# Attention then mixture of experts on one core: exponentials written in the order in which they are read, router lists with row and token apart

## The chip, the core and the metric

One core of a Trainium2 chip runs the whole program as one launch. The metric is the time of one execution in microseconds (us), as the device measures it. The engines are named as in the profile: PE (TensorE, matmuls), PEld (TensorE's weight loads), DVE (VectorE), ACT (ScalarE), POOL (GpSimd) and SP (SyncE, which here only issues DMAs). "Clock" is the granted clock of TensorE as a share of its upper level.

## The reference

Two parts, one behind the other. Attention: q and k are normalised by row (RMS with gains), then softmax(q k^T / 8) v for 8 batches of 12 heads, 448 positions, 64 numbers a head. Its output is laid out as 3584 tokens of 768 numbers. Then a mixture of 8 experts, of which each token goes to one:

```python
q_n, k_n = (rmsnorm(q, g_q), rmsnorm(k, g_k))
scores = scale * np.matmul(q_n, k_n.transpose(0, 1, 3, 2))
attn = np.exp(scores - np.max(scores, axis=-1, keepdims=True))
attn = attn / (np.sum(attn, axis=-1, keepdims=True) + 1e-09)
x = np.matmul(attn, v)   # 8, 12, 448, 64 -> 3584 tokens x 768
logits = x @ w_gate      # 8 experts, 448 tokens each, best logit first
for e in range(8):
    out[mask_e] = np.maximum(x[mask_e] @ w1[e], 0) @ w2[e]
```

## The kernel before

Attention works in 24 groups g of four heads (three groups make a batch of 12 heads). All its work is cut into tasks, and a task has one engine. `Plan.run` issues the tasks in the order of a long table of digits, `ORDER`; two tasks of one engine therefore run in the order of the table, whatever is ready first. A planner with task durations (`US`, in which an exponential has 0.917) made the table outside the program. Each task waits for its inputs by semaphores.

For a group, in order: SP loads q, k and v (`load_qk`, `load_v`); ACT squares (`square`, line 301) and DVE sums (307); ACT and POOL make the reciprocal roots (313 to 321); POOL normalises (342) and multiplies by the gains (371); ACT writes the upper halves of the numbers as f16 (376) and POOL the rest (379); SP issues two DMA transposes (389, upper halves into kqh, lower into kql). Then PE makes scores with the upper halves for the row maxima (`max_score`, 504; DVE reduces them, 514), small transposes of the maxima (444) go back as a row through a DMA (456), and PE makes the exact scores, transposed, keys on partitions (`scores`, 535 and 537; 542 and 544 for the first groups).

One unit d is a seventh of a group: 16 matmuls into the PSUM tile psc (128 x 896), then one exponential on ACT (`exp`, 553) from psc into the SBUF tile e (128 x 896 f32). There are 168 units. `av` (572) then uses 64-column pieces of e as weights and v as the moving operand; a call is one window w of seven, 8 matmuls in the program and 16 in the profile, since those in f32 show twice. There are 336 such windows. DVE and ACT normalise the result po (585 to 605) into xa, and once per batch SP stores xa to the DRAM scratch xd (`x_store`) and transposes it for the gate (612); gate matmuls (668 to 676) make the logits.

Groups 0 to 2 are loaded so that a partition holds three neighbouring tokens of a head, and groups from 3 on (`seven(g)`) so that a partition holds seven. A column 64 j + i of psc then is token 7 i + j. For these 147 units `exp` writes e through a view that puts column 64 j + i at place 7 i + j, so that neighbouring elements are written 28 bytes apart and e stands in token order. For the first 21 units input and output are both dense.

psc has two buffers, e has 15, kqh 4, kql 3. All exponentials run on ACT, beside squares, upper halves, part of v's copies and one of the steps on po.

`Router` places tokens. Its constants are made during attention on POOL and DVE (`later`); `tok` holds the token of each partition and column in two parts, number / 64 and the rest, since bf16 holds no more. Phase k fills the expert that is full at that point: `at`, `columns` and `rows` make one-hot operands, `lists` multiplies them on PE (28 matmuls of 8 columns) and two DVE instructions put the parts together to `idx`. `Experts.gather` reads rows of xd by idx (an indirect DMA on POOL), and `result` scatters its rows to the output by the same idx. Phase 0 stands between attention and the first expert; the others run beside the experts before.

Of the kernel before, what the change touches and what calls it, by code (L numbers as in the profile page):

```python
# [89 lines left out]
class Attention:  # L90
# [792 lines left out]
    def plan_first(self, plan, g, a):  # L883
# [51 lines left out]
        "Bw2bL-LyBxRBBy3fGu2F3M2dM22G2e2H2f3O3Q2g2IRCM4BzB+M6GvB-M5GxRD3g3hC0RERFC1M3M8M7C23N3P3i3j3k4M3R4NGw3+Gy3-C3Gz"
        "C4H140G+C5C6G-353637C7C8413l38H0H23m0A0B3n3o4243M9MBMFC9CAH5H3CBH4H6RGRHCCRIRJ4O4QMAMEMCCDCEMDRKH7H8CFCGH9HA3p"
        "44464548473Z3q3rMGCHMKMHMMML4RCICJ4P4SCKRLRMHB4THDHCHE3S3TMJCLHFMI4U49RNROCMCNHGRPRQCOHHHJCPRRCQRSMNMPMRCRCS4A"
        "4V4B3V4W4X3WHIHK4mRTRU583UHNHL3X4o4YHMCTCUMTMUMXCV4nCW5AHO4a4p4q3Y4rMQMaMOMW594CCXCYMSHP3sRVRW3t3uRXMYCZCaMVHR"
        "CbCcMZ3z5CRYHQHSHTCdRZRaRbCe5BHVHUHWMbMgCfCgRcHX4c4b3v4Z4D4dHZHYChCiMhMcMfCj5DCkHbRdHaHcReRhRjHdHe5E5FClCmMeMd"
        "Mi4E4F4G0C4s0DRtHfCnCoRuMoMjMmCpRvCq4u4t4w4v4x3x5Y4y4zHhHgHlCrCsHiRw3yRxMlMnMkRyCtCuHjHkHm3wMpMvCvMtMuMs5ZRzCw"  # L940
        "Cx5G5H5I5JR+CyHnHpR-5aHoS04e4f5bMrMqRl4+CzS1C+Hq5c5dHrHsRi5w5K5y5M4LRgRk5x4H4I5eHt4JHuC-D0S2MwMxMyD1D20rS3S4Mz"
        "M-N0D3D4HvHwS55L5NHxD5D6M+S65z4gRm4h5fHyHzH+D7D8S7S8H-RnRoRpD9DA4jI04KS9SAI1I2I35ODBDCRqN1N250514-Rf4k5iI5DDRr"
        "RsDEN3N8NDDF5g5hI45k5j0E5l4iDGI6NBN5NEDJDKI7I9DH5+5-6KI8IA606M61DIN4N6N7SBNA0FSCDLDMSDIBICSE526i5mIDDNDON9SFIF"
        "4lDPDQNCSG6L0G626465630H0I0J535654IEIGNFNHNI5QSH5RSISJIHIIDRDSSKNJIJ5P666768IKDTDU6N6ONGNKNLSZDVNMNQNRNO5n6j5S"
        "DWDXDYILINSaSbDZDa6P6k556mIMScSdIONSNPNN0K0L6Q6R69575T6S6TDbDc6nIPIR5WIQ6UIS5o5p6l6oNTNUNZSPSS6ADdITIU76DeSeSf"
        "SgShIV6p6WIW6XDfDgSiNYNXNWNVDhSjDiSkIXSRSQSTSVSUDjSlDkIZIYSmIbSnDlDmSWIa78SX77SYNaNgNcDnDoIdNb5V5UNhDp79Dq5qSL"
        "IcIe6YIfIhIg7AIiDrNeDs6B5X6q6V6s6r6tNfNkNd6CSo6DSpSq7B6u6wSr5r6xSO5vIj7U7V7W5tIk5uDtDuSsNlNnIlDxDyNoNjNpDvDwNm"
        "NiNqStDzInImIoIpD+SuSvSwD-E0SxNtNsIrE1Nr7XE25sNvNuSy6y7YIqNyNzN-6a6ESMSN6ZIt6v0M7C7D0N0O7E7u7G6J8G6z7F0P0Q7H6F"
        "SzS+S-Is6b6cT0T4T5T87I7KT6T7E3E46G0R6IN+NwNxO0O3TF7ZTGE5Iv6HIuIwTH7a7b7wTIE67vO4IxE7E8IzO5O2O1IyI+7x7yEBECI-J3"
        "E9J0TJEAO6J17J8H7LT2EDEETK7c0S7d7e8I7f6d6eJ2O7ODO8OAJ4EFJ56f7gJ68JTLTMTNO9J7EG6+6-T370J9EH7zJ8JA7i7k7j7h7+80TO"  # L950
        "EIOCOBTPTQTRTSJBEJEKJDT9TBTAELTTEMJCJEJFJHEPEQJGJI6gOETCOKOJENEO8KTDTEJLJJERESJKJM7-82818485OGOHOIOFETOLONOP6h"
        "718LEU8M8N8O0T0U72EVEWTUTVJN8gJOJPJQ7M7N9275T1937l7OTWOMEXEYTXTYOQJRJSEZOOOREaOSEbTZEcTaTb8i7374OTOUOYEdEeTcTd"
        "JTJV838P8Q8687Ef8ROVOWOX7PJU7SJW7ROZOfOeEgTe8hTfTgEhJZEiObOa7m7n7oJX8S8TTh8U8VJYJa94Ti7TTnTpTk8WEjEkOcOgOiOd8j"
        "TxTyElEmTzJbJcJdJeEnEoT+T-OhOjOkOlOmEpEq95U0JfJgJhErEsU1U27Q7p7s8k96Ji8l8m8oOnOoOqOrEtEuJjJkJlJmEvOpEwJp8889U3"
        "U4JnEx97EyOtOuOsOxOvO+U5EzU6U7E+Jo8nJq8p8q8sU89S8tU9JrJtJsJuE-F07tTqOzOyOw8BUAUBToTlTrTsTtUCF1F2JxUD98997r8EJv"
        "Jw9UUEF3Tu7q8rO-P0P3P4TvJyF49TTwF5P1F6P6P7F7F89q8XTj8A8uJzJ+8DJ-K0F99V9WFAP5PCP9P2FBFCUFUGK1K38F8v9r9A9B9C9E9D"
        "9GK2K48Y8Z8a9IPAUHFFFGK5K7FDUI9XUJFE9H8C9Y9a9FP8PBPDUKULUM9sK6K8PFFHFIUNUOUTUWUUKBK9KAKCFJFKPEPJPKFLFMKDKEKFFN"
        "FOPQKHKGKI9u8w8x8yTm8fUSKJKK9Z8b9c8d9b8e9eFPPGPOPPFQFRFS9tPHPMPIFVFWUdUeKLUfKNKMKOUgPNFTFUUhKRKPKQFXPL9d8c8z9f"
        "90KS8+9v9w9xFYPRPWPUPTFZUiUjFaKTKUUkUl8-KVKW9gFbFcAEUmPXPSPVUn9K9LUoKXFdKZ91UVUXUZUYUpFeFfUqUrUaUbPYPZPeFgKYUc"
        "FhFiAF9y9+9-9z0V0WAc9JA0A2Ad9hKaAGAeA19MA49RPfPjPiFjFkAHAIAJPdPbPcPa0X9NA3AKAM9OFlFmUsUtKbA5KdFnPgPlPkPhFoUu9i"  # L960
        "9jUR9kKcKeUvKfKgKhKiFpUxUyUwFqUzU+PmPsPrPnFrFsKjKlFtU-AfFuPoPpPqV0V1V2AgAhKk9P9QPtPwPuPyFvFwKnPxPz0YALANAOAQV3"
        "V40Z0a9lAiAjKmKo9n9m0bAPAk0c0d0eAlARAmAnFxFyKpKqB0KrKsFzF+UPUQPvVJP+Q1F-G0VKKtKvAS9pG1G2AoAp9oKuKwVLVMQ2Q0Q3A6"
        "A7B1VNKzKxG3G4V7V8V9VBVAQ4P-A9ABKyAqA8K+Q5Q7Q6QBVOVPVQG5G6K-L1VRACVSG9GAB2B3Q8QAQ9VTG7G8L0L2B4B5QCQFQEQDGBVUVV"
        "GCL3L5GDGEQGQIQHVWVXL4L6VCATAsGFVYVZGGL7L9L8LAAUAVVaVDVEVFGHGIVbVcLBLDGJVGB6B7ArB8AAB9ADAXAYAZLCAaBABCBDBBVHAW"
# [11 lines left out]
class Router:  # L976
# [23 lines left out]
    def __init__(self, ctx, tc, logits):  # L1000
# [61 lines left out]
        tok = c.tile([128, NT], I32, name="tok")  # L1062
        for b, n in ((0, 1), (1, 5), (6, 1), (7, 1)):
            i, m = self.column(b)
            later("P", 0.13, G.iota, tok[:, i:i + 3 * n].rearrange("p (b j) -> p b j", j=3),
                  pattern=[[448, n], [128 if b else 1, 3]], base=448 * b, channel_multiplier=1 if b else 3)
            if b in (0, 6):
                n = 1 if b else 3
                for h in range(2):
                    later("P", 0.13, G.iota, tok[64 * h:64 * h + 64, m:m + n], pattern=[[896, n]],  # L1070
                          base=448 * (b + h) + 384, channel_multiplier=1)
        part = c.tile([128, 2, NT], I32, name="tokp")
        later("D", 0.1, V.tensor_scalar, part[:, 0], tok, 6, None, op0=OP.logical_shift_right)
        later("D", 0.1, V.tensor_scalar, part[:, 1], tok, 63, None, op0=OP.bitwise_and)
        self.tok = c.tile([128, 2, NT], BF, name="tokb")
# [912 lines left out]
```

## Time and profile before

| | us |
|---|---|
| median of 3 runs (969.11 to 973.3) | 970.84 |
| the profiled execution | 970.76 |
| its span, first to last instruction | 968.7 |
| first exponential starts | 32.57 |
| last `av` matmuls start | 463.83 |
| first gather of rows starts | 493.56 |

Attention fills about the first 464 us, phase 0 of the router with little matmul work follows, and from 500 us on PE is busy nearly without a break with the experts. A row with a count ("x4") groups instructions of one kind that stand together. Matmuls are pipelined: the distance between two starts tells what PE needs for the work between them, and the duration of a row contains a tail in which the next one already runs.

### The profile page before, as it was taken

The numbers are of one execution on the slowest core, as the hardware profiler recorded it, in microseconds if no ns is written. First come the engines' busy times: TensorE is split into PE (matmuls) and PEld (weight loads), VectorE is DVE, ScalarE is ACT, GpSimd is POOL, SyncE is SP. The second block draws the span as 40 slices with busy tenths as digits, with TensorE's granted clock in tenths as the row PEclk, the third lists the DMA queues.
The fourth block names the chain that finished last, engine by engine and source line by source line (L and its number), as shares of the span: only waits on it lengthen the run. The fifth ranks groups of instructions, "written<-read, shape, count | busy, mean of one in ns | idle before, by whom it ended". The sixth has DMA issues, their size and how long they took to land.

```text
span 968.7 us, 30160 instructions
## 1 busy us (share of the span) xinstructions
PE 876.6 (90%) x13219; PEld 584.3 (60%) x13220; DVE 658.9 (68%) x1457; ACT 583.9 (60%) x670; POOL 342.8 (35%) x421
## 2 busy tenths in 40 slices
PE   2799889898998898888679999999999999999996
PEld 1466656675765676667555655556555565555783
DVE  6988777776776676653679677777775858338640
ACT  4889999999998999887224342434242414333421
POOL 6778656775745576510010202111101111020101
PEclk9999999999999999999679999999999999999999
DMA  6586869798896687391163756968684929660501
GB/s 190 151 169 151 178 132 214 174 222 166 180 197 146 116 204 153 58 223 26 60 219 100 234 174 196 236 193 224 197 212 149 268 81 293 222 139 8 181 17 41
DMA packets 224951, 157.30 MB, mean 162 GB/s; under 512 B 162100, under 2 KB 211508, under 8 KB 224820
## 3 DMA queue, kind: packets, MB, share of 16 engines
q1 hardware_dynamic: 219378, 132.90, 57.3%
q0 software_dynamic: 4608, 22.02, 6.6%
q8 instruction: 103, 1.69, 0.7%
q10 hardware_dynamic: 834, 0.46, 0.2%
q14 instruction: 28, 0.23, 0.1%
HBM read 94.40 MB, written 22.02 MB: 120 GB/s over the span
## 4 chain that ended last, share of the span: by engine, by line
issue 33%; PE 10%; POOL 5%; DVE 2%; DMA 0%; ACT 0%; POOLq 0%; DVEq 0%
PE ph L1765 6%; PE py L1782 3%; POOL out_dram L1798 3%; POOL rows L1702 3%; DMA rows<-xd,idx 0%; PE rp L1238 0%; POOL spacer L1797 0%; PE rp L1466 0%; PE rp L1309 0%; DVE or L1213 0%; DVE or L1459 0%; DVE cmp L1223 0%; PE py L1791 0%; PE py L1717 0%; ACT xt L1721 0%
## 5 line engine op out<-in xcount | busy, mean ns | idle before, releaser
L553 ACT ACTIVATE e<-psc 128x896 f32<-128x896 f32 x168 | 275.8, 1715 | 19.8 <-PE psc L537 15.7
L514 DVE TENSOR_REDUCE mx<-pm 128x2 f32<-128x896 f32 x162 | 176.6, 1090 | 69.4 <-PE pm L504 66.8
L572 PEld LDWEIGHTS po<-v,e 128*64 128x64 f32 x5376 | 168.5, 138 | 39.5 <-issue 33.1
L572 PE MATMUL po<-v,e 128*64 128x65 f32 x5376 | 185.9, 224 | 7.1 <-ACT e L553 2.6
L1765 PE MATMUL ph<-xt,w1h 128*128 128x448 f16 (+2 forms) x708 | 183.5, 343 | 0.4 <-DVE xt L1723 0.3
L1798 POOL DMA_INDIRECT out_dram<-y,idx x32 | 34.2, 1070 | 307.3 <-ACT y L1784 238.0
L1782 PE MATMUL py<-w2h,hh 128*128 128x384 f16 x384 | 125.0, 326 | 0.0
L1782 PE MATMUL py<-w2h,hl 128*128 128x384 f16 x384 | 125.0, 326 | 0.0
L1782 PE MATMUL py<-w2l,hh 128*128 128x384 f16 x384 | 125.0, 325 | 0.0
L1765 PE MATMUL ph<-xt,w1l 128*128 128x448 f16 (+2 forms) x354 | 119.9, 343 | 0.0
L1754 ACT ACTIVATE hh<-ph 128x448 f16<-128x448 f32 x56 | 30.5, 544 | 121.9 <-PE ph L1765 107.5
L1782 PEld LDWEIGHTS <-hh 128*128 128x128 f16 x768 | 73.6, 97 | 45.6
L1765 PEld LDWEIGHTS <-w1h 128*128 128x128 f16 x708 | 64.8, 97 | 52.7 <-issue 1.5
L1784 ACT ACTIVATE y<-py 128x384 f32<-128x384 f32 x48 | 23.5, 490 | 116.0 <-PE py L1782 92.5
L535 PE MATMUL psc<-kqh 64*64 64x448 f16 x588 | 56.2, 362 | 36.2 <-ACT e L553 33.1
L535 PEld LDWEIGHTS <-kqh 64*64 64x64 f16 x1176 | 44.1, 107 | 62.7 <-issue 49.0
L1702 POOL DMA_INDIRECT rows<-xd,idx x32 | 31.5, 986 | 115.4 <-DVE idx L1472 46.8
L1569 DVE SCALAR_TENSOR_TENSOR w2l<-stage,w2h 128x768 f16<-128x768 f32 x64 | 60.3, 952 | 10.7 <-ACT w2h L1565 10.6
L379 POOL TENSOR_TENSOR s<-qn,s 128x896 f16<-128x896 f32 (+2 forms) x25 | 44.6, 1786 | 47.5 <-ACT s L376 23.2
L504 PE MATMUL pm<-kqh 64*64 64x448 f16 x588 | 56.7, 364 | 2.5 <-DVE mx L514 2.1
L379 POOL TENSOR_TENSOR s<-kn,s 128x896 f16<-128x896 f32 (+2 forms) x25 | 44.7, 1787 | 34.2 <-ACT s L376 32.4
L307 DVE TENSOR_REDUCE st<-sq 128x14 f32<-128x910 f32 (+2 forms) x52 | 52.6, 1018 | 5.5 <-ACT sq L301 5.4
(301 smaller groups left out, 1640.2 us busy)
## 6 DMA issues: line engine op xcount, KB each, us to landing
stage<-in_moe_w_dram SPq DMA_DIRECT2D x64, 768.0 KB
vraw<-in_v_dram SPq DMA_DIRECT2D x21, 448.0 KB
xd<-xa SPq DMA_DIRECT2D x16, 576.0 KB
qkraw<-in_q_dram SPq DMA_DIRECT2D x10, 896.0 KB
qkraw<-in_k_dram SPq DMA_DIRECT2D x10, 896.0 KB
xd<-xa SPq DMA_DIRECT2D x16, 96.0 KB
vraw<-in_v_dram SPq DMA_DIRECT2D x3, 384.0 KB
qkraw<-in_q_dram SPq DMA_DIRECT2D x2, 384.0 KB
```

Of the source, the lines that this page charges most:

```text
L307: self.nc.vector.tensor_reduce(self.stat(g, 0, a)[:, i], self.view(self.T["sq", g, i], a), axis=AX.X, op=OP.add)
L379: self.tt("lo" + name, g, a)(self.half(g, 1, name, a), self.flat(self.T[name + "n", g], a), self.half(g, 0, name, a), op=OP.subtract)
L504: self.nc.tensor.matmul(o, mine, self.every(k, r, a), start=True, stop=True)
L514: self.nc.vector.tensor_reduce(m, p[r, :, :448], axis=AX.X, op=OP.max)
L535: mm(o, mine, self.every(q, r, n), start=i == 0, stop=False)
L553: self.nc.scalar.activation(e, p, AF.Exp, scale=scale)
L572: self.nc.tensor.matmul(po[o:o + 64, w], self.T["e", d][:, h, q:q + 64], self.v32[g % 2][:, h, 4 * a + d % 7 % 4], start=d == ds[0], stop= ...
L1569: self.later(0.93, lambda w=w: self.nc.vector.scalar_tensor_tensor(l[:, w], v[:, w], self.WS, h[:, w], op0=OP.mult, op1=OP.subtract), k, i)
L1702: nc.gpsimd.indirect_dma_start(out=g[:n, c, :], out_offset=None, in_=self.xd, in_offset=bass.IndirectOffsetOnAxis(ap=idx[:n, c:c + 1], axi ...
L1765: nc.tensor.matmul(p, a, b[:, o], start=st, stop=sp)
L1782: nc.tensor.matmul(p, a[:, f, s], b[:, f, o], start=st, stop=sp)
L1798: st = nc.gpsimd.indirect_dma_start(out=self.out, out_offset=bass.IndirectOffsetOnAxis(ap=self.router.idx[k][:n, c:c + 1], axis=0), in_=y[ ...
```

## The change

`exp` loses its view: all 168 exponentials read psc and write e in psc's own order. For groups from 3 on, place 64 j + i of e now holds token 7 i + j, so xa and the rows of xd stand in that order. For batch 0, `x_store` writes rows in the form of the other batches. So the row of a token in xd is no longer its number. `tok` therefore holds two lists, row and token (four parts), made by 20 iotas in place of 9; `columns` makes a one-hot and one product over all four parts in place of two products; the matmuls of `lists` have 16 columns in place of 8, and two more DVE instructions make a second list. `gather` goes by the row, `result` by the token. `ORDER` is a new table, since tasks were added.

```diff
@@ exp
-        p = p[:, :, :448]
-        if self.seven(d // 7):
-            e, p = e.rearrange("p h (i j) -> p h j i", j=7), p.rearrange("p h (j i) -> p h j i", j=7)
-        self.nc.scalar.activation(e, p, AF.Exp, scale=scale)
+        self.nc.scalar.activation(e, p[:, :, :448], AF.Exp, scale=scale)
@@ x_store
-            o = xd[:384].rearrange("(j p) (h c) -> p j h c" if b else "(p j) (h c) -> p j h c", j=3, h=2)
+            o = xd[:384].rearrange("(j p) (h c) -> p j h c", j=3, h=2)
@@ ORDER
-        "030500040708090n0v0x0w0y0o0p0602110z0-0+101213141Q151R16171S181A01191B1T1U1C1V1D1W2l1t1s1r1u1y2K1w1v1+1P1Y1X1E"
+        "050204031506160z1718191A0+1B0708000-1C1E1G1c1F1H1d1I1J1e1K1f1L091g1h1i1N1D1b1M011P1R242122252326281k1j1O1Q2x2z"
...
@@ Router.__init__
-        tok = c.tile([128, NT], I32, name="tok")
+        tok = c.tile([128, 2, NT], I32, name="tok")
...
-        later("P", 0.2, G.tensor_copy, self.tok, part)
+        later("D", 0.1, V.tensor_scalar, part[:, :, 0], tok, 6, None, op0=OP.logical_shift_right)
+        later("D", 0.1, V.tensor_scalar, part[:, :, 1], tok, 63, None, op0=OP.bitwise_and)
+        self.tok = c.tile([128, 4, NT], BF, name="tokb")
+        later("P", 0.3, G.tensor_copy, self.tok, part.rearrange("p n i t -> p (n i) t"))
@@ columns
-            V.tensor_tensor(oa[:, 0], ar[:, 0, :, None].to_broadcast([128, NT, 4]),
+            V.tensor_tensor(one, ar[:, 0, :, None].to_broadcast([128, NT, 4]),
                             self.row[:, None, 0:4].to_broadcast([128, NT, 4]), op=OP.is_equal)
-            for i in (1, 0):
-                V.tensor_tensor(oa[:, i], oa[:, 0], self.tok[:, i, :, None].to_broadcast([128, NT, 4]), op=OP.mult)
+            some = [128, 4, NT, 4]
+            V.tensor_tensor(oa, one[:, None].to_broadcast(some), self.tok[..., None].to_broadcast(some), op=OP.mult)
@@ lists
-            q = p[:, 0:8].rearrange("p (i a) -> p i a", i=2)
+            q = p[:, 0:16].rearrange("p (i a) -> p i a", i=4)
...
-            lo = self.small("idlo", [128, 4])
-            V.tensor_copy(lo, q[:, 1])
-            idx = self.idx[k] = self.w.tile([128, 4], I32, name="idx", bufs=8)
-            V.scalar_tensor_tensor(idx, q[:, 0], 64.0, lo, op0=OP.mult, op1=OP.add)
+            for n, of in enumerate((self.idx, self.out)):
+                lo = self.small("idlo", [128, 4])
+                V.tensor_copy(lo, q[:, 2 * n + 1])
+                idx = of[k] = self.w.tile([128, 4], I32, name=f"idx{n}", bufs=8)
+                V.scalar_tensor_tensor(idx, q[:, 2 * n], 64.0, lo, op0=OP.mult, op1=OP.add)
@@ result
-            out=self.out, out_offset=bass.IndirectOffsetOnAxis(ap=self.router.idx[k][:n, c:c + 1], axis=0),
+            out=self.out, out_offset=bass.IndirectOffsetOnAxis(ap=self.router.out[k][:n, c:c + 1], axis=0),
```

ACT in the middle of attention, around the third batch's gate (lsc is its part on ACT, s1 the f16 halves, st the roots, sq the squares), before:

```order
L553 ACTIVATE e_4527<-psc_4443 128x2x7x64
L553 ACTIVATE e_4529<-psc_4466 128x2x7x64
L553 ACTIVATE e_4571<-psc_4531 128x2x7x64
L553 ACTIVATE e_4573<-psc_4548 128x2x7x64
L467 ACTIVATE v32_1_139<-vraw_1_135 64x2x3x64
L301 ACTIVATE sq_1_137<-qkraw_3986 128x14x64
L707 ACTIVATE lsc_4620<-po_4483 128x24
L708 ACTIVATE lsc_4620<-po_4483 64x8
L553 ACTIVATE e_4665<-psc_4642 128x2x7x64
L553 ACTIVATE e_4667<-psc_4625 128x2x7x64
L376 ACTIVATE s1_4671<-kn_4669 128x896
L376 ACTIVATE s1_4671<-qn_4418 128x896
```

The same place now:

```order
L596 ACTIVATE xa_4120<-po_4220 128x7x64
L550 ACTIVATE e_4550<-psc_4516 128x896
L301 ACTIVATE sq_0_136<-qkraw_4403 128x14x64
L550 ACTIVATE e_4604<-psc_4533 128x896
L704 ACTIVATE lsc_4606<-po_4471 128x24
L705 ACTIVATE lsc_4606<-po_4471 64x8
L301 ACTIVATE sq_1_137<-qkraw_4403 128x14x64
L301 ACTIVATE sq_0_136<-qkraw_4403 128x14x64
L550 ACTIVATE e_4658<-psc_4630 128x896
L376 ACTIVATE s1_4660<-kn_4412 128x896
L376 ACTIVATE s1_4660<-qn_4414 128x896
L550 ACTIVATE e_4669<-psc_4613 128x896
```

The exponentials have lost their four-dimensional form, which in the first 21 units they never had, and stand singly between the other tasks where four stood in a row. On PE the table still has 168 units, 336 windows of `av` and 169 + 1 steps for maxima; the windows stand in 109 blocks where they stood in 112.

DVE in phase 0 (oa, or: the one-hot operands; idlo, idx: the list; tsel, newly, done: the tokens just placed), before:

```order
L1451 TENSOR_TENSOR oa_9476<-ar_9473,rowb_72 128x112
L1454 TENSOR_TENSOR oa_9476<-oa_9476,tokb_95 128x112 x2
L1459 TENSOR_TENSOR or_9109<-ar_9473,rows4_9129 128x2048
L1459 TENSOR_TENSOR or_9109<-ar_9473,rows4_9129 128x1536
L1470 COPY idlo_9511<-rp_9482 128x4
L1472 SCALAR_TENSOR_TENSOR idx_9513<-rp_9482,idlo_9511 128x4
L1415 SCALAR_TENSOR_TENSOR tsel_9515<-rp_9457,X_9427 128x28
```

The same place now:

```order
L1460 TENSOR_TENSOR oneh_9489<-ar_9485,rowb_72 128x112
L1463 TENSOR_TENSOR oa_9488<-oneh_9489,tokb_95 128x448
L1468 TENSOR_TENSOR or_9121<-ar_9485,rows4_9141 128x2048
L1468 TENSOR_TENSOR or_9121<-ar_9485,rows4_9141 128x1536
L1480 COPY idlo_9523<-rp_9494 128x4
L1482 SCALAR_TENSOR_TENSOR idx0_9525<-rp_9494,idlo_9523 128x4
L1480 COPY idlo_9527<-rp_9494 128x4
L1482 SCALAR_TENSOR_TENSOR idx1_9529<-rp_9494,idlo_9527 128x4
L1424 SCALAR_TENSOR_TENSOR tsel_9531<-rp_9469,X_9439 128x28
```

Two products of 112 elements became one of 448, and the second list (idx1) stands behind the first (idx0), on which alone the gather depends by data.

## Rows read from the trace of the kernel before

**Rows 1.** Windows: start:end, length, busy PE, PEld, DVE, ACT, POOL, clock, DMA share, GB/s.
```profile
57.00:94.00 37.00, 35.77 (x848) 25.94 (x841) 32.38 (x46) 33.43 (x44) 30.61 (x29) 1.00 0.80 176
94.00:460.00 366.00, 321.68 (x7810) 240.53 (x7809) 243.88 (x379) 341.82 (x336) 201.03 (x226) 0.99 0.77 160
460.00:500.00 40.00, 26.85 (x509) 19.64 (x511) 28.30 (x109) 8.21 (x16) 5.25 (x13) 0.66 0.33 107
500.00:968.00 468.00, 459.94 (x3576) 278.58 (x3574) 307.86 (x858) 163.56 (x203) 64.05 (x91) 1.00 0.58 169
```

**Rows 2.** Line 553, all exponentials: shortest, median and longest in ns.
```profile
L553 ACT ACTIVATE e<-psc x168: 898/1822/1903, 32.6 to 458.6; 128x896 f32<-128x896 f32 x168
```

**Rows 3.** Timeline of ACT: a pair of early exponentials, a pair of later ones.
```profile
62.20 1.73 ACT L553 ACTIVATE e<-psc 128x896 f32<-128x896 f32 x2
...
231.63 3.44 ACT L553 ACTIVATE e<-psc 128x896 f32<-128x896 f32 x2
```

**Rows 4.** Waits of PE from 57 to 464 us: total, times, longest.
```profile
PE psc L535 <- ACT e L553: 33.1, 47, 2.2
PE po L572 <- ACT e L553: 2.6, 6, 0.9
...
PE pm L444 <- DVE mx L514: 0.2, 1, 0.2
```

**Rows 5.** Timeline of PE where nothing waits: start, duration, instruction.
```profile
64.92 0.38 PE L504 MATMUL pm<-kqh 64*64 64x448 f16 x4
65.13 0.36 PE L542 MATMUL psc<-kqh 64*64 64x448 f16 x4
...
65.89 0.36 PE L542 MATMUL psc<-kqh 64*64 64x448 f16 x4
...
68.92 0.38 PE L504 MATMUL pm<-kqh 64*64 64x448 f16 x4
69.23 0.69 PE L572 MATMUL po<-v,e 128*64 128x65 f32 x16
69.85 0.38 PE L542 MATMUL psc<-kqh 64*64 64x448 f16 x4
...
72.60 2.09 PE L572 MATMUL po<-v,e 128*64 128x65 f32 x64
74.62 0.38 PE L504 MATMUL pm<-kqh 64*64 64x448 f16 x4
```

**Rows 6.** Windows, from 57.45 us, of line 572 alone (`av`): PE busy, PEld busy.
```profile
57.45:465.00 407.55, 179.18 (x5200) 162.77 (x5200) 0.99 0.76 160
```

**Rows 7.** The same of line 542 (scores of the first 21 units).
```profile
57.45:465.00 407.55, 8.89 (x144) 4.15 (x144) 0.99 0.76 160
```

**Rows 8.** The same of line 507 (scores for the first groups' maxima).
```profile
57.45:465.00 407.55, 0.49 (x8) 0.11 (x4) 0.99 0.76 160
```

**Rows 9.** The same of line 444 (maxima turned).
```profile
57.45:465.00 407.55, 6.94 (x88) 5.70 (x88) 0.99 0.76 160
```

**Rows 10.** The same of line 668 (gate).
```profile
57.45:465.00 407.55, 7.26 (x126) 6.60 (x126) 0.99 0.76 160
```

**Rows 11.** Timeline of PE: the last `av` matmuls.
```profile
463.83 0.28 PE L572 MATMUL po<-v,e 128*64 128x65 f32 x4
```

**Rows 12.** Windows, columns as in the first group, the 100 us with most DMA.
```profile
200.00:300.00 100.00, 88.68 (x2198) 66.83 (x2196) 70.78 (x106) 96.74 (x99) 64.74 (x73) 1.00 0.94 192
```

**Rows 13.** DMA transposes into kql on SP's queue: shortest, median, longest in ns.
```profile
L389 SPq DMA_TRANSPOSE kql<-s x22: 1508/2622/8285, 42.4 to 421.6; - x22
```

**Rows 14.** Timeline of phase 0's listing and what follows it on DVE and POOL.
```profile
489.06 0.59 DVE L1454 TENSOR_TENSOR oa<-oa,tokb 128x112 bf16<-128x112 bf16 x2
...
492.51 0.16 DVE L1472 SCALAR_TENSOR_TENSOR idx<-rp,idlo 128x4 int32<-128x4 f32 x1
...
493.56 1.18 POOL L1702 DMA_INDIRECT rows<-xd,idx  x1 [22.39 <-DVE gone L1422]
...
497.50 0.62 DVE L1295 TENSOR_TENSOR cmp<-v,rows 128x896 bf16<-128x896 bf16 x1
```

More of the change, by code (lines that the diff above doesn't have):

```diff
@@ L935 @@
[L935 to L964, printed above, removed]
@@ L970 @@
+        "LnGpGqQuQwQsGrB7B9BAWEWFGsLmLoLpLrLqBSQtBTQvWJWKB8QxR0QyR1Q-Q+QzBPBRW0BUV+VzBBWLLtWMWSWTWNLsLuWULvW5W7W6LwWVWW"
+        "BVLzLxX3W8W9WABYLyL+BXR2R6R7R3R5R4R8L-M1WGM0M2WaWbWcWdWeM5M3M4WHM6BWR9RFRERARCRBRGRLRKRJRDRMRIRHWjWkWlWrWsWtWm"
+        "WnWOWQWuWPWXWfWhWYWvWIW-X0WRWxWoWZWgWiX1WpWqX2W+WyWzWw"
     )
@@ L1060, in __init__ @@
         later("P", 0.12, G.memset, self.xs[:, 0:1], 0.0)
-        tok = c.tile([128, NT], I32, name="tok")
+        tok = c.tile([128, 2, NT], I32, name="tok")
         for b, n in ((0, 1), (1, 5), (6, 1), (7, 1)):
             i, m = self.column(b)
[L1065 to L1075, printed above, removed]
-        later("P", 0.2, G.tensor_copy, self.tok, part)
+            main = lambda t: t[:, i:i + 3 * n].rearrange("p (b j) -> p b j", j=3)
+            later("P", 0.13, G.iota, main(tok[:, 0]), pattern=[[448, n], [128, 3]], base=448 * b, channel_multiplier=1)
@@ new lines, in __init__ @@
+            if b == 0:
+                later("P", 0.13, G.iota, main(tok[:, 1]), pattern=[[448, n], [1, 3]], base=0, channel_multiplier=3)
+                later("P", 0.13, G.iota, tok[:64, 1, m:m + 1], pattern=[[1, 1]], base=384, channel_multiplier=1)
+                later("P", 0.13, G.iota, tok[:64, 1, m + 1:m + 3], pattern=[[896, 2]], base=902, channel_multiplier=7)
+                later("P", 0.13, G.iota, tok[64:, 1, m:m + 3], pattern=[[896, 3]], base=454, channel_multiplier=7)
+            for h in range(2):
+                o = tok[64 * h:64 * h + 64]
+                if b:
+                    later("P", 0.13, G.iota, main(o[:, 1]), pattern=[[448, n], [2, 3]], base=448 * b + h,
+                          channel_multiplier=7)
+                if b in (0, 6):
+                    n_ = 1 if b else 3
+                    later("P", 0.13, G.iota, o[:, 0, m:m + n_], pattern=[[896, n_]], base=448 * (b + h) + 384,
+                          channel_multiplier=1)
+                if b == 6:
+                    later("P", 0.13, G.iota, o[:, 1, m:m + 1], pattern=[[896, 1]], base=448 * (b + h) + 6,
+                          channel_multiplier=7)
@@ L1078, in __init__ @@
+        part = c.tile([128, 2, 2, NT], I32, name="tokp")
+        later("D", 0.1, V.tensor_scalar, part[:, :, 0], tok, 6, None, op0=OP.logical_shift_right)
+        later("D", 0.1, V.tensor_scalar, part[:, :, 1], tok, 63, None, op0=OP.bitwise_and)
+        self.tok = c.tile([128, 4, NT], BF, name="tokb")
+        later("P", 0.3, G.tensor_copy, self.tok, part.rearrange("p n i t -> p (n i) t"))
         self.placed = c.tile([128, NT], F32, name="placed")
@@ L1088, in __init__ @@
         self.e = {}
-        self.idx = {}
+        self.idx, self.out = {}, {}
         self.oh = c.tile([128, 8, NT], BF, name="oh")
@@ L1448, in columns @@
         def columns():
-            oa, ar = self.small("oa", [128, 2, NT, 4], BF), st["ar"]
+            oa, one, ar = self.small("oa", [128, 4, NT, 4], BF), self.small("oneh", [128, NT, 4], BF), st["ar"]
             st["oa"] = oa
-            V.tensor_tensor(oa[:, 0], ar[:, 0, :, None].to_broadcast([128, NT, 4]),
+            V.tensor_tensor(one, ar[:, 0, :, None].to_broadcast([128, NT, 4]),
                             self.row[:, None, 0:4].to_broadcast([128, NT, 4]), op=OP.is_equal)
-            for i in (1, 0):
-                V.tensor_tensor(oa[:, i], oa[:, 0], self.tok[:, i, :, None].to_broadcast([128, NT, 4]), op=OP.mult)
+            some = [128, 4, NT, 4]
+            V.tensor_tensor(oa, one[:, None].to_broadcast(some), self.tok[..., None].to_broadcast(some), op=OP.mult)
         def rows(h):
```

43 lines of the change are left out of this document (35 added, 8 removed).

## Prediction

> **What bounds the kernel now.** I first cut the span into stages by the windows view [rows 1]. From 500 us on PE is busy 459.94 of 468 us: the experts are bound by matmuls, and nothing in this part of the change touches them. From 460 to 500 us a chain of small steps on DVE runs. The stage that the change can move is attention. From 94 to 460 us ACT is busy 341.82 of 366 us (93%), PE 321.68 (88%), DVE 243.88 (67%), POOL 201.03 (55%), and the DMA engines 77%. So ACT is nearest to its limit, with PE close behind.
>
> Then I looked at what ACT does. The exponential of one and the same shape takes 898 ns at the shortest and 1822 at the median [rows 2]. The timeline tells the two kinds apart: an early pair takes 1.73 us together, a later pair 3.44 [rows 3]. The early ones belong to the first 21 units, which write densely; the later ones, 147 units, write 28 bytes apart. The waits view agrees that this is felt: from 57 to 464 us, PE waited 33.1 + 2.6 us for exponentials, of 45.2 in all its 11 rows [rows 4].
>
> The stretch from 57 to 94 us is the most useful one. Nearly all of it has dense exponentials, and there PE is busy 35.77 of 37 us, though DVE (32.38) and POOL (30.61) are fuller than ever after [rows 1]. That is attention without the slow exponential: bound by PE. What the change can give is thus set by PE's own work, not by what ACT is relieved of.
>
> **The exponentials.** Each of 147 becomes like the early ones: (3.44 - 1.73) / 2 = 0.855 us less, and 147 x 0.855 = 125.7 us less on ACT. From 57 to 460 us ACT then has 33.43 + 341.82 - 125.7 = 250 us of work, DVE 276 and POOL 232 as before [rows 1]. PE's work I count from starts where nothing waits [rows 5], since busy time contains overlapping tails:
>
> - A unit's scores: 65.89 - 65.13 = 0.76 us. Left at 57.45 us: 144 / 12 = 12 early units [rows 7] and the 147 others, 159 x 0.76 = 120.8 us.
> - The scores for maxima: about 0.2 us (65.13 - 64.92, with 0.01 for the start). Left: 8 / 4 = 2 [rows 8] and 147, 149 x 0.2 = 29.8 us.
> - `av`: one window (16 rows) 69.85 - 69.23 = 0.62, four windows (64) 74.62 - 72.60 = 2.02, so (2.02 - 0.62) / 3 = 0.467 for a window and 0.15 for a block; and the step into a block costs 0.31 (69.23 - 68.92) where otherwise 0.2, so 0.26 for each block. Left: 5200 / 16 = 325 windows [rows 6], 151.8 us, and some 105 of 112 blocks, 27.3 us. The new table has 109 blocks, three fewer, 0.8 us that I leave out.
> - Maxima turned 6.9 [rows 9] and gates 7.3 [rows 10], busy times.
>
> The sum is 120.8 + 29.8 + 151.8 + 27.3 + 14.2 = 343.9 us. It began at 57.5 and ended with the last `av` at 463.8 [rows 11], that is 406.3 us; so 62.4 us were lost. 45.2 of them are the waits listed; the other 17.2 I put down to the part of each wait that hides under a modelled tail, and to little else. This closes well enough to go by it.
>
> What will stay of the 62.4? Waits that were not for exponentials, 45.2 - 35.7 = 9.5, with their share of the hidden part, 17.2 x 9.5 / 45.2 = 3.6: 13.1 us. I take all of it, since a new table at a higher rate will have its own misfits: 13.1 of 344 is 4%, and in the stretch from 57 to 94 us PE idled 1.23 of 37 us, 3%. So the last `av` ends at 57.5 + 343.9 + 13.1 = 414.5 us, 49.3 us earlier. The bounds: with no wait at all 62.4 us; and, where the rest becomes the limit, see the second case below. ACT's time no longer sets anything then; next are PE, and the DMA engines with 0.80 x 37 + 0.77 x 366 = 311 us of shares in the same stretch.
>
> [...] If the order of writing cost nothing, the view's removal would be worth nothing; that is a case below.
>
> **Lists.** Two products of 112 elements took 0.59 us; one of 448 lies between 0.28 (half of that) and 0.62, the row of 896 elements [rows 14], so -0.3 to +0.03; I take 0. The matmuls with 16 columns for 8 I take at nothing: 28 of them, and no row here depends on so few columns. Two more DVE instructions of 0.16 us [rows 14] stand behind the first list and ahead of what the gather was seen to be released by (the row that names "gone"), so 0.3 us later, in the first phase on the path; in the seven others under matmuls. If the gather waits for its list alone, they cost nothing. I take +0.3. Behind them on DVE wait the updates for the next phase, which PE's first expert covers.
>
> **Constants, stores, start.** Eleven more iotas go to POOL; even at the longest POOL row shown, 1.18 us [rows 14], 13 us, against 344 - 232 = 112 us free. Stores of batch 0 write pieces of the same size. The order of the first loads differs: PE is not full before 57 us, and I allow 3 us either way, and take 0.
>
> **Sum.** 970.76 - 49.3 + 0.3 = **921.8 us** for the profiled execution; the median of the runs shown is 970.84, 0.08 more, which I leave out.
>
> **Rivals.**
>
> 1. *Transfers set the rate.* The share of 311 us has to fit in 357 us, a mean of 0.87. For: over 100 us a share of 0.94 is the most that was sustained [rows 12], and SP's transposes wait in one queue for their inputs. Against: in that very stretch PE ran no slower than elsewhere. If only the 0.80 of 57 to 94 us can be held, attention from there takes 389 us, the last `av` ends at 446.5, 17.3 us are gained: 953.8 us. At 0.85, 366 us and 931. I put this case at 931 to 954, 14%.
> 2. *Hardly a wait stays*: 62.4 us gained, 908.7 us. For: the early stretch. Against: no table fits as well over 340 us. 908 to 915, 8%.
> 3. *PE has room.* From 94 to 460 us the weight loads were busy 240.53 of 366 us, 66% [rows 1]; if PE could be packed until they are full, transfers would be the limit, 311 / 0.94 = 331 us, the last `av` at 388.5, 75.3 gained: 895.8 us. [...] Against it: starts without a gap [rows 5] in a stretch where weight loads took 25.94 / 37 = 70% [rows 1], so full PE looks like this here. 3%.
> 4. *The long exponential does not come from the writes* (but, say, from psc's place or a later time in the run): nothing gained, 971 us. Against: shape, function and source are the same, and only the output's view differs. 3%.
> 5. *Slower: SP's queue starves PE.* Transposes stand in SP's queue in the order of the new table, behind loads that wait for buffers; one took 8.29 us there against 2.62 at the median [rows 13]. If in each of 22 groups such a delay was not covered by the lead of the maxima over the scores, 22 x 5.67 = 125 us are lost against 49 gained: some 1046 us. It decides from 49.0 / 22 = 2.2 us a group upwards. For: one queue in fixed order, at a rate 1.14 times as high. Against: no row of PE's waits names a transfer today. 4%.
>
> **How the numbers follow.** The first forecast has 68%, between 915 and 931. To hold 8 in 10, I add the case of hardly a wait and the nearer half of the transfers: 908 to 941 us. Faster by over 0.5% (about what a measurement of this kernel can tell from no change): cases 1, 2, 3 and the forecast, 93%; within 0.5%: case 4, 3%; slower: case 5, 4%.
>
> **What would show it.** Right: all exponentials near 0.9 us; the last `av` near 414 us; in the windows of attention PE 95% or more, ACT near 70%; PE's waits for e a few us; the distance from the last `av` to the first gather as before, within 1 us; 500 us to the end as before. Case 1 shows as a DMA share over 0.9 with PE, DVE and POOL all waiting for kqh, kql or loads; case 5 as PE's gaps ended by transposes. What would make it wrong is a new wait of more than some 0.6 us in each group (13 us over 22 groups), wherever it comes from.

## The result

The changed kernel took **920.14 us** (median of 4 runs, 916.3 to 921.92) beside 972.04 us for the kernel before (4 runs): a ratio of 0.9465, 95% interval 0.9426 to 0.9503. The forecast was 921.8 us. The profiled execution took 916.3 us, the fastest of the four; its span is 914.5 us.

All exponentials are now of the short kind. The line's own view, shortest, median and longest in ns, against [rows 2]:

```profile
L550 ACT ACTIVATE e<-psc x168: 891/916/939, 34.6 to 405.7; 128x896 f32<-128x896 f32 x168
```

The page's group for that line, busy time, mean in ns, then idle time before and what ended it:

```profile
L550 ACT ACTIVATE e<-psc 128x896 f32<-128x896 f32 x168 | 148.6, 912 | 49.9 <-PE psc L537 39.3
```

ACT now waits for PE (39.3 us for scores), where PE had waited for ACT. The windows of the changed kernel, columns as in [rows 1]:

```profile
57.00:94.00 37.00, 35.70 (x848) 25.80 (x840) 32.79 (x48) 28.80 (x41) 31.38 (x32) 1.00 0.73 181
94.00:411.00 317.00, 311.94 (x7978) 239.36 (x7975) 244.80 (x382) 231.27 (x343) 202.45 (x236) 1.00 0.92 186
...
447.00:914.00 467.00, 458.77 (x3553) 277.38 (x3549) 309.60 (x861) 162.48 (x203) 64.08 (x91) 1.00 0.57 169
```

In attention PE is busy 98% (88% before), ACT 73% (93% before), the DMA engines 92% (77% before). Behind attention little changed: from the last `av` to the first gather 28.9 us (29.7 before), and from there to the end of the span 475.0 us (475.1 before). The waits of PE from 57 to 420 us, in total, times, longest, against [rows 4]:

```profile
PE po L569 <- issue: 2.8, 5, 1.3
PE pm L504 <- DMA kqh<-s: 1.4, 1, 1.4
...
PE psc L535 <- ACT e L550: 0.4, 1, 0.4
```

The 33.1 + 2.6 us of waits for exponentials are down to 0.4. The `av` matmuls, first and last start at the end of the time part:

```profile
L569 PE MATMUL po<-v,e x5376: 217/222/272, 44.8 to 410.6; 128*64 128x65 f32 x200
```

The last ones start at 410.6 where they started at 463.83 [rows 11]: 53.2 us earlier, of the 54.5 us between the two profiled executions. So attention accounts for nearly the whole gain.

### The profile page after: what moved, and what is told of

Read it like the earlier page. It is cut to its first block, busy times and chain, and to the rows that moved or that the text cites. A ratio compares the mean times of both kernels' runs of the same rounds, so it can differ in the third digit from the quotient of the medians.

```text
span 914.5 us, 30177 instructions
## 1 busy us (share of the span) xinstructions
PE 863.1 (94%) x13219; PEld 579.4 (63%) x13220; DVE 660.6 (72%) x1465; ACT 466.9 (51%) x670; POOL 343.0 (38%) x433
## 4 chain that ended last, share of the span: by engine, by line
PE 71%; issue 17%; DVE 5%; POOL 3%; DMA 2%; ACT 1%; SPq 1%; POOLq 0%; DVEq 0%
PE po L569 18%; PE ph L1775 16%; PE py L1792 13%; PE psc L535 9%; PE pm L504 4%; PE psc L537 3%; PE py L1801 2%; DVE mx L514 2%; POOL out_dram L1808 1%; POOL rows L1712 1%; DMA kqh<-s 1%; PE psc L542 1%; PE rp L1318 1%; DVE st L307 1%; PE rp L1475 1%
## 5 line engine op out<-in xcount | busy, mean ns | idle before, releaser
L569 PEld LDWEIGHTS po<-v,e 128*64 128x64 f32 x5376 | 166.8, 137 | 31.8 <-issue 28.9
L569 PE MATMUL po<-v,e 128*64 128x65 f32 x5376 | 182.6, 223 | 2.9 <-issue 2.8
L550 ACT ACTIVATE e<-psc 128x896 f32<-128x896 f32 x168 | 148.6, 912 | 49.9 <-PE psc L537 39.3
L537 PE MATMUL psc<-rowq,rowk 64*64 64x448 f16 x588 | 55.8, 349 | 0.7 <-issue 0.7
L1766 DVE SCALAR_TENSOR_TENSOR hl<-ph,hh 128x448 f16<-128x448 f32 x56 | 34.1, 617 | 30.9 <-ACT hh L1764 30.8
L535 PE MATMUL psc<-kql,kqh 64*64 64x448 f16 x588 | 55.4, 349 | 0.0
```

What stands on the lines that cost most here:

```text
L535: mm(o, mine, self.every(q, r, n), start=i == 0, stop=False)
L537: mm(o, one[r, :64], self.every(row, r, n), start=False, stop=True)
L550: self.nc.scalar.activation(e, p[:, :, :448], AF.Exp, scale=scale)
L569: self.nc.tensor.matmul(po[o:o + 64, w], self.T["e", d][:, h, q:q + 64], self.v32[g % 2][:, h, 4 * a + d % 7 % 4], start=d == ds[0], stop= ...
```

## The experiments

Each run is compared with runs of the kernel before on the same chip. The medians of that kernel lie between 972.0 and 973.9 us there, so a difference of 1 or 2 us between two runs says nothing. A waits row gives one execution, the profiled one.

**1. What makes an exponential long.** In the changed kernel the 168 exponentials take turns in eight forms of writing and reading; psc and the function stay. The parts that follow are not rearranged, so e has other orders.

```diff
@@ exp
+        far = lambda t, n: t.rearrange("p h (i j) -> p h j i", j=n)
+        near = lambda t, n: t.rearrange("p h (j i) -> p h j i", j=n)
-        self.nc.scalar.activation(e, p[:, :, :448], AF.Exp, scale=scale)
...
+        elif n == 3:
+            act(far(e, 7), near(p, 7), AF.Exp, scale=scale)
...
+        elif n == 6:
+            act(near(e, 7), far(p, 7), AF.Exp, scale=scale)
...
```

The forms, by n = d % 8: dense; written 8, 16, 28 and 56 bytes apart and read in a row; dense in four dimensions; read 28 and 16 bytes apart and written in a row. The first 21 units stay dense.

> The changed kernel with the exponentials of groups 3 to 23 in eight forms by turns, each on a line of its own: dense as in the changed kernel; written 8, 16, 28 and 56 bytes apart; dense on both sides but in the four-dimensional form; written densely but read from PSUM 28 and 16 bytes apart. (Rows of attention are permuted and the output is not the reference's; the work is the same.) My theory, distance of the writes: dense 0.91 us in either form, 28 and 56 bytes 1.8 us, 16 bytes 1.8 or a little under, 8 bytes between 0.9 and 1.8; reads at a distance 0.9. Rival, the form: the dense four-dimensional one takes 1.8 too. Rival, distance on either side: reads 28 and 16 bytes apart take 1.8.

The lines in the order of the eight forms:

```profile
L555 ACT ACTIVATE e<-psc x39: 895/917/924, 33.9 to 405.5; 128x896 f32<-128x896 f32 x39
L557 ACT ACTIVATE e<-psc x18: 949/988/1019, 96.4 to 406.3; 128x896 f32<-128x896 f32 x18
L559 ACT ACTIVATE e<-psc x18: 1766/1818/1868, 97.3 to 409.9; 128x896 f32<-128x896 f32 x18
L561 ACT ACTIVATE e<-psc x18: 1777/1819/1876, 99.3 to 411.5; 128x896 f32<-128x896 f32 x18
L563 ACT ACTIVATE e<-psc x18: 1688/1750/1799, 100.9 to 413.9; 128x896 f32<-128x896 f32 x18
L565 ACT ACTIVATE e<-psc x19: 896/919/988, 86.7 to 415.4; 128x896 f32<-128x896 f32 x19
L567 ACT ACTIVATE e<-psc x19: 895/917/920, 89.5 to 417.5; 128x896 f32<-128x896 f32 x19
L569 ACT ACTIVATE e<-psc x19: 894/917/926, 93.3 to 419.0; 128x896 f32<-128x896 f32 x19
```

Among these forms only the distance of the *writes* costs: 8 bytes 0.07 us, 16, 28 and 56 bytes 0.83 to 0.90. The dense view in four dimensions is free (0.919 us against 0.917), and so is reading PSUM 28 and 16 bytes apart (0.917 both). (The run as a whole took 929.66 us, in one execution.)

**2. One part alone.** Either the kernel before with the dense exponential and nothing else, or the changed kernel with the 28-byte writes back. In both, e's order does not fit what follows, so the rows of x come out permuted.

```diff
@@ exp, in the kernel before (e1; reversed in the changed kernel: e2)
-        p = p[:, :, :448]
-        if self.seven(d // 7):
-            e, p = e.rearrange("p h (i j) -> p h j i", j=7), p.rearrange("p h (j i) -> p h j i", j=7)
-        self.nc.scalar.activation(e, p, AF.Exp, scale=scale)
+        self.nc.scalar.activation(e, p[:, :, :448], AF.Exp, scale=scale)
```

> The kernel before with one edit: all exponentials write densely. Old order table, old lists (so the rows of groups 3 to 23 come out permuted; the amount of work is the reference's). My theory, the writes alone are the gain: 922 us, 916 to 928, the last av near 413 us. Rival, the new order table brings the gain or a good part of it: 940 to 971 us.

> The changed kernel with one edit: groups 3 to 23 write their exponentials 28 bytes apart again. New order table, new lists (rows permuted, work the same). My theory: all of the gain is lost, 971 us, 964 to 980, and PE waits 30 us and more for exponentials again. Rival, the new order: 945 us or less.

The dense exponential alone: 926.03 us (924.9 to 928.76), ratio 0.9515 (0.9475 to 0.9555). All but the dense exponential: 969.51 us, ratio 0.9958 (0.994 to 0.9976), and PE waits for exponentials again, as the waits from 57 us on show:

```profile
PE psc L535 <- ACT e L553: 30.5, 45, 1.8
PE po L572 <- ACT e L553: 3.4, 4, 1.1
```

So the writes carry nearly all of the gain. Some 6 us lie between the dense exponential in the old table and in the new one (926.0, 920.1). The intervals of the two ratios overlap, but each of the four runs with the old table took longer than each of the four with the new one; experiment 5 takes that up.

**3. The same relief without moving anything else.** In the kernel before, the view is turned round: e is written in a row in token order, and psc is read 256 bytes apart. Nothing else changes.

```diff
@@ exp
-            e, p = e.rearrange("p h (i j) -> p h j i", j=7), p.rearrange("p h (j i) -> p h j i", j=7)
+            e, p = e.rearrange("p h (i j) -> p h i j", j=7), p.rearrange("p h (j i) -> p h i j", j=7)
```

> The kernel before with one edit: the exponentials of groups 3 to 23 write densely in token order and read psc 256 bytes apart instead, so that no other part needs to change and the output is the reference's. If only the distance of the writes costs: 922 us, 916 to 928, and an exponential takes 0.92 us. If a distance costs alike on both sides: 971 us, an exponential 1.8 us. Between: by 147 times the excess over 0.92 us, as far as that exceeds what PE hides, so no loss up to about 1.2 us an exponential.

930.11 us (924.49 to 934.19), ratio 0.9535 (0.9481 to 0.959). The exponentials, though they read 256 bytes apart:

```profile
L553 ACT ACTIVATE e<-psc x168: 893/917/924, 32.0 to 416.6; 128x896 f32<-128x896 f32 x168
```

New rows in xd and a second list are not needed for the gain. A table of order, to fit the shorter exponentials, is what is left to explain.

**4. What bounds the changed kernel.** PE's work is raised and lowered by one pass of score matmuls (27.9 us of PE, an estimate from [rows 5]: 147 x 0.76 / 4), and the loads by 8.5 MB.

```diff
@@ scores (f1 adds a pass; f2 leaves one out)
-            for i, (k, q) in enumerate(((kh, qh), (kl, qh), (kh, ql))):
+            for i, (k, q) in enumerate(((kh, qh), (kl, qh), (kh, ql), (kl, ql))):   # f1
+            for i, (k, q) in enumerate(((kh, qh), (kl, qh))):                       # f2
@@ load_v (f3: groups from 5 on use the v of groups 3 and 4; g1: f2 and f3)
+        if g >= 5:
+            return
```

> The changed kernel with a fifth pass of scores in groups 3 to 23, lower halves of k by lower halves of q: 4 matmuls of 0.19 us together for each of 147 units, 27.9 us of PE work, nothing else. (The output stays the reference's.) My theory, PE sets the pace: 920 + 27.9 = 948 us, 944 to 951. Rival, transfers set it (their share is 0.96 from 94 to 400 us): PE's work hides under them, 920 to 934 us.

> The changed kernel without one pass of scores in groups 3 to 23, upper halves of k by lower halves of q, so the scores are less exact: 27.9 us less of PE work. If PE alone sets the pace: 892 us. What I expect: PE's work from 57 us falls to some 316 us, near the 320 us of shares of the transfers, so these begin to bind and only part is gained: 895 to 910 us. Rival, transfers already set it: 917 to 921.

> The changed kernel without the loads of v from group 5 on (the two buffers keep the v of groups 3 and 4, so the output is not the reference's): 19 transfers of 448 KB less, some 8.5 MB. My theory: the transfers' share from 94 to 400 us falls from 0.96 to about 0.87 and the time moves little, 915 to 920 us, by the few microseconds in which PE waited for late transposes. Rival, transfers set the pace: the time falls by their share, 19 x 1.5 = 28 us, to 892 us.

More work cost 19.3 us (939.44, 937.6 to 941.26), less work gave 7.6 us (912.56, 909.91 to 916.66), fewer loads 3.7 us (916.39, 915.11 to 918.03; the interval of its ratio, 0.9389 to 0.9421, lies just below that of the changed kernel). The first two came out closer to the changed kernel than expected. With the last `av` at 434.2 (f1), 410.6 (changed) and 402.0 us (f2), and PE's own work, counted as in the prediction, at 372.9, 345 and 317.1 us from 57.45 us on, PE lost about 4, 8 and 27 us (one execution each, the slowest of f1 and the fastest of the other two). f2 has a limit of its own. Its waits of PEld and PE from 57 to 420 us:

```profile
PEld L504 <- issue: 13.9, 42, 0.7
PEld L504 <- DMA kqh<-s: 8.9, 3, 5.5
...
PE pm L504 <- DMA kqh<-s: 7.9, 3, 5.0
```

In the changed kernel the first of these rows is small:

```profile
PEld L504 <- issue: 0.8, 2, 0.5
```

The 13.1 us more (13.9 - 0.8), and 6.5 us more (7.9 - 1.4) for kqh, add up to about what f2 did not gain: 27.9 - 13.1 - 6.5 = 8.3, and its last `av` came 8.6 us earlier. Other rows moved too (PEld's waits before `av` fell from 27.9 to 21.6 us, those for mx at line 444 rose from 0.6 to 4.7), so this sum is a hint and no proof. At first I took the transfers for the limit. The run with both cuts tells:

> The changed kernel without TensorE's score pass kh x ql (27.9 us of TensorE's work, as in f2_less_pe) and without the loads of v from group 5 on (8.5 MB, as in f3_less_v; the v of groups 3 and 4 is used again): both parts of the computation are left out, so its time is that of less work. f2_less_pe took 27.9 us of TensorE's work away and gained 7.5 us; f3_less_v gained 3.7 us. If the transfers are what f2_less_pe ran into, the two together gain far more than the 11.2 us of their sum: 893 to 902 us, with no wait of TensorE for kqh. If another engine or the order stops it (VectorE's, GpSimd's or ScalarE's share of the key-tile steps), it stays at 907 to 912 us and TensorE's waits name that engine.

907.92 us (901.87 to 911.48), ratio 0.9312 (0.9258 to 0.9367). The median stayed where the other engines would hold it, though one of the four runs, 901.87, lies in the range for the transfers. Window from 94 to 390 us in the changed kernel, and then with both cuts, with its waits of PEld and PE:

```profile
94.00:390.00 296.00, 290.94 (x7382) 221.84 (x7380) 236.32 (x355) 219.97 (x325) 201.14 (x234) 1.00 0.97 194
```

```profile
94.00:390.00 296.00, 282.31 (x6993) 213.60 (x6983) 236.50 (x361) 221.64 (x327) 201.94 (x236) 0.99 0.89 169
...
PEld L506 <- issue: 13.7, 42, 0.5
...
PE pm L506 <- DMA kqh<-s: 5.4, 2, 2.7
```

The DMA share fell to 0.89 and the 42 small waits stayed (13.7 us). So did 5.4 of the 7.9 us of waiting for kqh: fewer loads do not take that away, and what makes those transposes late was not tested. What the 42 small waits are, the timeline of f2 shows (start, duration, instruction, idle time before it):

```profile
202.80 0.38 PE L504 MATMUL pm<-kqh 64*64 64x448 f16 x4
...
203.23 1.09 DVE L514 TENSOR_REDUCE mx<-pm 128x2 f32<-128x896 f32 x1 [0.23 <-PE pm L504]
...
203.96 0.11 PEld L504 LDWEIGHTS <-kqh 64*64 64x64 f16 x1
...
204.38 0.38 PE L504 MATMUL pm<-kqh 64*64 64x448 f16 x4
204.38 0.11 PEld L504 LDWEIGHTS <-kqh 64*64 64x64 f16 x3 [0.32 <-issue]
```

There is one PSUM tile pm (the ring has one buffer). Its maximum is read from 203.23 to 204.32; one weight load is already done, and the next matmuls into pm start at 204.38. DVE stood idle for 0.23 us before this maximum, so here it is the length of the maximum that counts and not DVE's other work. So in f2 the reading of pm by DVE, 1.09 us, paces PE wherever two maxima have little between them. Halving that instruction tests it:

```diff
@@ max_reduce, in f2
-        self.nc.vector.tensor_reduce(m, p[r, :, :448], axis=AX.X, op=OP.max)
+        self.nc.vector.tensor_reduce(m, p[r, :, :224], axis=AX.X, op=OP.max)
```

> f2_less_pe (the changed kernel without TensorE's score pass kh x ql) with VectorE's maxima of the scores taken over 224 of the 448 columns, which leaves half of each maximum's columns out and makes its instruction about half as long (1.09 us in f2_less_pe). In f2_less_pe TensorE loaded weights for a maximum late 42 times, 13.9 us together, since there is one PSUM tile pm and VectorE had not yet read the maxima before; the wait for kqh is 7.9 us. If VectorE's hold on pm is what f2_less_pe ran into, those 42 small waits go and it comes to 898 to 903 us (912.6 less 10 to 14). If the transfers or ScalarE are, it stays at 909 to 914 us with the other waits grown.

902.06 us (898.73 to 910.92, 6 runs), ratio 0.9269 (0.9242 to 0.9295): 10.5 us below f2, as expected. The maxima, and what is left of the waits of PE and PEld in the profiled execution (the slowest of the six):

```profile
L514 DVE TENSOR_REDUCE mx<-pm x162: 602/626/629, 21.8 to 374.4; 128x2 f32<-128x448 f32 x162
...
PE pm L504 <- DMA kqh<-s: 7.9, 4, 4.3
...
PEld L504 <- issue: 1.7, 6, 0.5
```

Of the 42 waits 6 are left, 1.7 us together; those for transposes stay, in this execution at least. So the changed kernel is bound by PE, and close below lie first the one buffer pm with DVE's 1.09 us on it, then late transposes of kqh. A second buffer for pm was not tried.

**5. What the new table is worth.** The old table with the dense exponential loses 6 us. Late transfers were one suspect.

```diff
@@ load_v, in e1
+        if g >= 5:
+            return
```

> The kernel before with the dense exponential alone (e1_old_order_dense, 926.0 us) and without the loads of v from group 5 on (8.5 MB; the v of groups 3 and 4 is used again), which leaves part of the computation out. If the old table of the order loses its 6 us against the changed kernel because transposed loads of q and k come late behind other transfers, it comes down to 917 to 921 us and the gaps of 2 to 4 us before TensorE's line 504 are gone. If the loss is in the order of TensorE's own work, it stays at 922 to 926 us with the gaps in place.

922.41 us (921.73 to 927.21): 3.6 us less than e1 by the medians (the intervals of the ratios overlap), as much as the changed kernel gained from the same cut (3.7). So transfers do not explain the difference between the tables. The other gaps of over 2 us are down to 1.6; one stayed:

```profile
PE pm L506 <- DVE mx L516: 4.2, 1, 4.2
```

The timeline of e1 around it, start, duration, instruction:

```profile
123.06 1.89 POOL L379 TENSOR_TENSOR s<-qn,s 128x896 f16<-128x896 f32 x1
123.20 1.80 DVE L178 TENSOR_SCALAR wg<-wg 128x48 f16<-128x48 f32 x1
...
124.90 0.61 POOL L469 COPY v<-vraw 64x512 f32<-64x512 f32 x1
125.04 3.83 DVE L179 SCALAR_TENSOR_TENSOR wg<-wg,wg 128x48 f16<-128x48 f32 x1
...
125.47 1.69 POOL L342 TENSOR_TENSOR kn<-qkraw,st 128x896 f32<-128x896 f32 x1
127.11 1.68 POOL L342 TENSOR_TENSOR qn<-qkraw,st 128x896 f32<-128x896 f32 x1
...
129.32 1.07 DVE L514 TENSOR_REDUCE mx<-pm 128x2 f32<-128x896 f32 x1
...
130.45 0.58 PE L504 MATMUL pm<-kqh 64*64 64x448 f16 x4 [4.45 <-DVE mx L514]
```

Two instructions on 128 x 48 numbers hold DVE for 5.6 us. The first ends at 125.00, when POOL's product has ended (124.95); the second at 128.87, after a copy and two more products (128.79). The maximum stands behind them (and behind one step on po), and PE waits 4.45 us for it. In the profile of experiment 3 the same two take 1.79 and 3.83 us, and PE waits 3.1 us. In e1 PE's clock is lower after the wait, as the windows show (the number before the DMA share is the granted clock: 0.53 and 0.52, then 1.00):

```profile
130.40:132.00 1.60, 1.55 (x20) 1.07 (x19) 1.45 (x2) 1.20 (x2) 0.55 (x1) 0.53 1.13 241
132.00:134.00 2.00, 2.00 (x26) 1.01 (x28) 1.32 (x3) 0.21 (x1) 0.00 (x0) 0.52 0.70 252
134.00:136.00 2.00, 2.00 (x64) 1.39 (x60) 1.83 (x3) 1.95 (x3) 0.00 (x0) 1.00 0.00 0
```

By an estimate from these rows 3.6 us at 0.53 and 0.52 cost another 1.7 us; if the lower clock comes from the wait (in h2, further down, without the wait, the clock is 1.00 from 126 to 138 us), this one place is worth some 6.2 us. In the changed kernel POOL is idle at that point:

```profile
108.15 0.18 DVE L178 TENSOR_SCALAR wg<-wg 128x48 f16<-128x48 f32 x1
108.36 0.21 DVE L179 SCALAR_TENSOR_TENSOR wg<-wg,wg 128x48 f16<-128x48 f32 x1
...
108.78 1.89 POOL L379 TENSOR_TENSOR s<-qn,s 128x896 f16<-128x896 f32 x1 [5.36 <-ACT s L376]
```

To test it, POOL does this step itself, in the old table, once with the dense exponential of e1 (h2), once with that of experiment 3 (i1).

```diff
@@ gate_weights
-            nc.vector.tensor_scalar(self.wg[:, :, 0:8], wg32, self.WS, None, op0=OP.mult)
-            nc.vector.scalar_tensor_tensor(self.wg[:, :, 8:16], wg32, self.WS, self.wg[:, :, 0:8], op0=OP.mult,
-                                           op1=OP.subtract)
+            G.tensor_scalar(self.wg[:, :, 0:8], wg32, self.WS, None, op0=OP.mult)
+            G.tensor_scalar(wg32, wg32, self.WS, None, op0=OP.mult)
+            G.tensor_tensor(self.wg[:, :, 8:16], wg32, self.wg[:, :, 0:8], op=OP.subtract)
```

> e1_old_order_dense (the kernel before with the dense exponential alone) with the two small VectorE instructions that split the gate's weights (lines 178 and 179, 128x48) done by GpSimd instead. In e1_old_order_dense they took 1.80 and 3.83 us while GpSimd ran its products, against 0.18 and 0.21 us in the changed kernel where GpSimd was idle, and TensorE waited 4.45 us for the maximum queued behind them; its clock fell after that. If this stall is most of what the old table loses against the changed kernel, the time goes from 926.0 to 920 to 922 us and the wait of 4.45 us at 130 us is gone. If the later gaps of 2.2 and 2.4 us swallow it, it stays at 924 to 927 us.

> e3_read_apart (the kernel before, whose later exponentials write densely and read 256 bytes apart: rows, lists and table of the order as before) with the gate's weights split by GpSimd as in h2_old_order_wg_pool; nothing is left out. If the stall behind the two small VectorE instructions was what the old table lost, it comes from 930.1 to 918 to 925 us, as good as the changed kernel (920.1) without its new table, its second list and its new rows. If reading 256 bytes apart or the old rows cost something of their own, it stays at 926 to 930 us.

h2 took 918.82 us (917.85 to 922.02), ratio 0.9454 (0.9433 to 0.9475): the loss of the old table is gone, and the time is within the changed kernel's interval (and meets e1's only at its end, 0.9475). The step's three instructions take 0.34, 0.33 and 0.28 us on POOL, and no wait for mx is left among PE's longer ones:

```profile
L178 POOL TENSOR_SCALAR wg<-wg x1: 341/341/341, 119.1 to 119.1; 128x48 f16<-128x48 f32 x1
...
PE po L569 <- issue: 5.4, 6, 1.6
PE pm L504 <- issue: 1.6, 1, 1.6
```

i1, which needs neither the new rows nor the second list nor the new table, took 922.71 us (921.02 to 926.76), ratio 0.95 (0.9477 to 0.9524). This interval overlaps with that of the changed kernel and with that of experiment 3, so its place between them is not fixed. Its last `av` starts at 411.3 us, as early as in the others; the few us more lie in the experts, where PE waits once, before 600 us, in its profiled execution:

```profile
PE ph L1765 <- issue: 3.4, 1, 3.4
```

The profile of experiment 3 has the same wait (3.1 us); those of h2, e1, the kernel before and the changed kernel do not have it. So it was seen only where the exponentials read 256 bytes apart; what ends it the profile does not show, and it stays open.

## Why the prediction was right

**The exponentials.** 0.855 us was predicted for each of 147. ACT's busy time on the line went from 275.8 to 148.6 us, 127.2 less (forecast 125.7). That it is the writes was a premise taken from a pair of rows; experiment 1 shows it, and experiment 2 that the gain hangs on it. Rival 4 is out.

**PE's own work.** The forecast put 343.9 us of work and 13.1 us of waits between 57.5 us and the last `av`. By the same count, what is left in the changed kernel at 57.45 us is about 345 us (160 units, 150 maxima, 326 windows); the last `av` starts at 410.6 instead of 414.5, so that about 8 us were lost. This profiled execution is the fastest of four, and the median, 920.14, lies 1.7 us under the forecast: 13.1 was a little too much or nearly right, depending on the run. The premise that the stretch from 57 to 94 us shows attention without slow exponentials held: PE is busy 96% there (35.70 of 37 us) and 98% after it (311.94 of 317).

**The term I had argued most weakly** was that the waits which were not for exponentials stay as they are. Their sum came out about right, but not for that reason, which is luck. Of those 9.5 us, 7.8 (line 504's waits for mx, and those for st, xa and logits) are gone in the changed kernel, and others stand in their place: 2.8 us before `av`, where it was 1.1, and 1.4 for kqh. And with shorter exponentials the old table gets a stall of 4.45 us in one place, and the new table does not have it. The forecast did not see it: in the kernel before, the two instructions on wg took 0.65 and 1.83 us and nobody waited long. That the new table has POOL idle there is, as far as the forecast goes, luck too: such a stall costs some 6 us, by the estimate under experiment 5.

**Lists: +0.3 forecast, 0.0 measured.** The timeline of phase 0 after, as in [rows 14]:

```profile
434.94 0.62 DVE L1463 TENSOR_TENSOR oa<-oneh,tokb 128x448 bf16<-128x448 bf16 x1
...
438.42 0.16 DVE L1482 SCALAR_TENSOR_TENSOR idx<-rp,idlo 128x4 int32<-128x4 f32 x1
...
438.81 0.16 DVE L1482 SCALAR_TENSOR_TENSOR idx<-rp,idlo 128x4 int32<-128x4 f32 x1
...
439.26 0.18 DVE L1430 TENSOR_TENSOR placed<-smax,mark 128x28 f32<-128x28 bf16 x1
...
439.46 1.18 POOL L1712 DMA_INDIRECT rows<-xd,idx  x1 [22.05 <-DVE placed L1430]
```

The first list ends at 438.58 and the gather starts 0.88 us later; before, 492.67 and 493.56, 0.89 us. "Placed" starts 0.68 us behind the end of the first list, 0.29 us before the change, and the gather did not move with it. The gather thus waits for its own list alone, and neither "placed", named here, nor "gone", named before, releases it. The second list ends 0.49 us ahead of the gather. The one product took 0.62 us, the upper end; its two predecessors 0.59. (Half of that is 0.30, not 0.28 as the forecast has it; and the trace has 8 iotas for tok before and 20 after, so twelve more and not eleven. Neither moves the sum.)

**Rival 1, transfers set the rate,** failed by its own marks: the share is over 0.9, as it asked, but PE hardly waits for transfers. A share of 0.94 was the most seen [rows 12], and the changed kernel holds 0.97 from 94 to 390 us with 1.4 us of PE's waits for kqh. Fewer loads give 3.7 us, so transfers are felt, but they are not the rate. **Rival 5** (SP's queue) has the same 1.4 us against it. **Rival 2** (hardly a wait) came nearest: the profiled execution alone, 916.3 us, lies between it and the forecast. **Rival 3**: the weight loads were busy 239.36 of 317 us (76%), so PE does pack denser than the 66% before, and than the 70% of the early stretch, on which the argument against it rested. But no room was left behind it: 27.9 us more of PE's work cost 19.3. By the 76% alone a quarter of the time would be left; this trace has 8 of 353 us.
